# Attention scores of a three-layer kernel: blocks of 32 queries by 96 keys in place of 64 by 128

## The chip, the cores and the metric

One core of a Trainium2 chip runs the whole kernel. The metric is the device time of one execution in microseconds; three executions of the kernel before gave 797.9, 798.71 and 799.32 us, and their median, 798.71 us, is what the change is held against.

## What is computed

The input of two MLP layers is the result of an attention with a sliding window. There are 4 batches, 8 heads, 576 positions and 64 features a head; each position sees itself and the 63 positions before it.

```python
scores = np.matmul(q, k.transpose(0, 1, 3, 2)) / np.sqrt(64)
rel = pos[:, None] - pos[None, :]
scores = np.where((rel >= 0) & (rel < 64), scores, -1e9)
attn = np.exp(scores - scores.max(-1, keepdims=True))
attn = attn / (attn.sum(-1, keepdims=True) + 1e-09)
x = (attn @ v) laid out as [2304, 512]
h = x @ w_in1;  g = np.maximum(h, 0) + alpha * np.minimum(h, 0);  x = g @ w_out1
h = x @ w_in2;  g = h / (1 + np.exp(-h));                         out = g @ w_out2
```

## The kernel before

The 2304 rows are cut into six tiles of 384 rows. The attention works in 24 items: one item is one tile of 384 rows and one pair of heads, whose two times 64 features fill the 128 partitions of `qT` and `kT` (`kT` has 64 keys more, ahead of the tile). An item goes through these functions:

- `mm_s` (S in the opening list, line 212): the scores. For each block of 64 queries (six of them) and each head of the pair there is one fp32 matmul with 64 rows (the features), 64 columns (the queries) and 128 moving columns (the keys from 64 before the block to its end). Each fp32 matmul shows as two instructions in the trace, so an item has 24. The two heads' results lie on the two halves of the partitions (`side`), and even and odd blocks lie in two PSUM banks.
- `peaks` (m, line 223): on VectorE, for each half of an item three instructions that add the mask, scale, write the probabilities' buffer `pr` and take the row's extreme. The bank of a half is given back after its three.
- `exps` (e, line 237): on ScalarE, three exponentials for each half, each with a sum along the row.
- `over` (r) and `scaled` (s): the reciprocal of the sums, and the multiplication by it, on GpSimd (P at the end of the word), ScalarE (A) or VectorE.
- `mm_t` (t, line 272) and `keep_t` (k): three 128 by 128 transposes for each half, and the copy out of PSUM into `pt`.
- `mm_v` (P, line 290): for each of the six blocks and each head one fp32 matmul with 128 rows (the keys), 64 columns (the features of `v`, tiles `vo` and `ve` in turn) and 64 moving columns (the queries): 12 matmuls, 24 instructions.
- `high_v`, `low_v` (x, l): the result is split into two fp32r parts, the input of the first MLP.

The first MLP's first product (`mlp_h1`, M, line 392) takes three fp32r matmuls of 384 columns for each of four 128-row pieces. All items of the first 14, and all M of the first two tiles, stand in an order written out by hand, the string `START`: each word is one call, and the words are issued in that order on every engine's queue (line 811). Among them are q, v and w (loads of queries and keys, of values, of weights), c, h and o (weights taken apart), z (`alpha_in`, line 131: the load of alpha on SyncE's queue, then one VectorE instruction that waits for it), G and J (the MLP's activation).

After the opening the other ten items are done two at a time, every eighth step of the first MLP's loop, in `begin` (line 1052), with five PSUM banks; `soft` spreads their softmax over the next steps. From there on the kernel is the two MLPs alone.

Before the list GpSimd builds the identity and the mask (lines 114 to 127), and for the items 0 to 3 it or VectorE clears the first 64 keys of `kT` (lines 173 and 180: item 0 on VectorE, the others on GpSimd). Keys of the first three items that the list loads go out on ScalarE's queue (line 169), and item 0 is loaded in two halves.

Of the kernel before, what the change touches and what calls it, by code (L numbers as in the profile page):

```python
# [20 lines left out]
q0 q1 q2 S0 m0a S1 e0a q5 q4 m0b e0b r0aP s0aP m1a e1a m1b S2 S5 e1b r0b m2a q3 r1aP m2b e2a r1b s0bP q8 s1bP s1aP t0b  # L21
S3 e2b m5b m5a t1b k0bD m3b q7 v0 S4 e5a r2bP m3a s2bP v1 v2 v5 t0a k1bD m4a r5aP r2aP t1a e5b k1aD k0aD r5bP e3a e4a
S7 S8 m7a e3b e7a t2b s5aP s2aP m8a t5a m4b q6 v6 v4 w12 q9 P0 r3aP r4aP k5aD x0 k2bD s5bP P1 t5b s3aP x1 t2a m7b t3a
e4b k2aD r3bP r7aP S6 s4aP s3bP e7b m8b l0 k5bD P2 t4a m6a s7aP k3a t3b r4bP k3bD t7a r7bP l1 q10 w13 m6b c12a P5 e6a
k7aD s4bP s7bP k4a c12b r6aP P3 t4b c12c t7b e6b r6bP k7b S9 S10 s6aP k4b m9b P7 x5 x3 x2 m10b P4 t6a h12 l2 s6bP t6b
l3 l5 o12 e8a e8b k6b m9a k6aD w3 r8aP w2 z e9a q11 q12 r8bP M0.12.1 M0.12.2 v8 M1.12.1 s8a s8bP P6 m10a x4 c3a x6 t8a
c2a r9a e9b x7 t8b l4 M0.12.3 l6 r9b M0.12.0 l7 s9aP k8a c2b M1.12.0 k8b s9bP t9a e10a c3b c2c r10a M1.12.2 M1.12.3
t9b P8 G1.12 G0.12 k9a S12 S11 c3c v9 k9b h2 h3 J0.12 J1.12 P9 m11a e11a s10aP t10a m11b m12b e11b o2 x9 M0.2.2 M0.2.1
w11 v10 w15 x8 c11a o3 w9 c11b r11a M1.2.1 c13a M1.2.3 M1.2.0 s11a M1.2.2 M1.3.3 M1.3.1 r11b M0.2.3 e10b M0.2.0 M1.3.0
M1.3.2 s11bA v11 q13 l9 r10bP s10bA t10b k10a c11c c9a c13b c9b t11a t11b c15a h11 k10b m12a P10 l8 o11 k11a w14 S13  # L30
c9c k11b P11 w5 c13c h13 m13a c14a x10 x11 M1.11.0 m13b G0.2 c14b M0.3.1 M1.11.2 c15b M0.11.3 l10 M0.3.2 c15c G1.3 h9
v13 w6 M1.11.1 o13D M1.11.3 o9 c14c w7 h15 M1.9.3 l11 M1.9.0 M1.9.2 M0.3.0 v12 w4 M0.3.3 M0.9.1 G1.11 G1.2 G0.3 J1.11
h14 J1.3 J1.2 M1.13.3 o15 M0.11.0 M0.11.2 c6a c5a J0.3 c5b c6b o14 M0.15.1 c4a M1.13.0 M0.15.3 M1.13.1 c5c h5 c4b
M1.9.1 c7a G1.9 M0.15.2 c4c M0.13.2 c7b J0.2 o5D M1.14.2 J1.9 M0.15.0 M1.14.3 M1.13.2 M1.14.1 M0.9.3 G0.15 G1.13 w0 w8
c6c w10 c7c M0.13.0 h7 o7 w1 M1.14.0 J0.15 c0a G1.14 M0.5.1 h4 M0.9.0 h6 J1.14 M0.5.3 M1.15.2 M0.13.1 e13a M1.15.1
M0.5.2 M1.7.1 c10a M1.15.0 M0.14.3 M0.11.1 c10b J1.13 M0.13.3 M1.15.3 M0.9.2 o4 M0.5.0 M1.7.0 G0.13 o6 G0.5 c1a J0.13
c1b G0.11 J0.5 M0.14.2 M1.5.0 M1.7.3 c10c c8a c1c M0.14.1 c8b G0.9 c8c G1.15 M0.14.0 M0.7.2 M1.5.3 M1.5.1 h1 M0.6.1
J0.9 o1D M0.7.1 c0b J1.15 M0.6.2 c0c M1.7.2 M1.5.2 G0.14 h10 J0.11 e12a o10D G1.5 G1.7 e13b h0 h8 o0D M1.4.3 M1.4.2
M0.7.3 J0.14 e12b M0.10.0 M0.4.0 M0.6.0 o8 J1.5 M1.4.1 J1.7 M1.4.0 M1.0.1 M0.6.3 M0.8.2 M0.4.1 G1.4 M0.7.0 M0.4.3
M1.0.3 M1.0.0 M1.0.2 r12a r12bP r13a G0.7 M1.6.1 J1.4 G1.0 G0.6 M1.8.1 M0.8.3 J1.0 M1.1.0 J0.6 M0.10.2 M0.1.3 M1.1.2  # L40
M1.8.0 M0.1.0 M0.1.2 M1.1.1 M1.8.3 M0.1.1 M0.10.3 M1.1.3 J0.7 G0.1 M1.6.0 G1.1 M0.0.0 r13bP M0.4.2 s12bP J1.1 J0.1
M1.8.2 M1.6.3 M1.10.3 M0.0.1 M0.10.1 s13aP G1.8 s12a G0.10 J1.8 J0.10 M0.0.2 M0.8.1 M1.6.2 M0.0.3 M0.8.0 M1.10.1 G0.4
M1.10.0 J0.4 G1.6 G0.0 G0.8 J1.6 J0.0 M1.10.2 s13bP J0.8 G1.10 J1.10
"""


B11, T3, B21, T2, T4, B22, T1 = range(7)
A11, S3, A12, S2, A22, S4, S1, A21 = range(8)
# [3 lines left out]
def attention_two_mlps(ctx, tc, q, k, v, w_in1, w_out1, alpha, w_in2, w_out2, out):  # L52
# [999 lines left out]
    def begin(s, n):  # L1052
# [144 lines left out]
```

## Time and profile before

| | us |
|---|---|
| median of three executions | 798.71 |
| the profiled execution, its time | 800.73 |
| its span, first to last instruction | 798.9 |
| TensorE matmul busy | 787.3 |
| VectorE busy | 631.6 |
| ScalarE busy | 489.3 |
| GpSimd busy | 125.3 |

The profiled execution took 2.0 us (0.25%) more than the median, and 1.8 us of its time lie around the span. Matmuls overlap in the array, and the ends that the profile gives them are modelled; so the length of one says little, and the distance from one start to the next says what it costs. PEclk is the clock that TensorE was granted, as a share of 2.4 GHz.

### The profile page before, as it was taken

Reading aid. Unit: us, or ns where it says so; the run is one execution under the profiler, and the core shown is the slowest. Engines: PE = TensorE matmul, PEld = TensorE weight load, DVE = VectorE, ACT = ScalarE, POOL = GpSimd, SP = SyncE. Lnnn points to the kernel's source line nnn. Section 1 sums busy time; section 2 is a strip of 40 time slices with the busy share of each in tenths; the row PEclk is TensorE's granted clock in tenths of the full one; section 3 lists DMA queues with packets and bytes.
Section 4 is the critical chain, followed back from the end, with each engine's and each line's share of the span. In section 5 each row is a group of like instructions: output and inputs, shape, how many; then the busy total and the mean of one; then the engine's idle time right before and its main releaser. Section 6 shows DMA issues by size and latency. Waiting matters only on the chain.

```text
span 798.9 us, 16657 instructions
## 1 busy us (share of the span) xinstructions
PE 787.3 (99%) x5475; PEld 756.1 (95%) x5475; DVE 631.6 (79%) x1611; ACT 489.3 (61%) x1301; POOL 125.3 (16%) x165
## 2 busy tenths in 40 slices
PE   7899999999999999999999999999999999999998
PEld 6799999999999999999999999999999888888887
DVE  6896647788878998978889775865984988968876
ACT  7873446776734576564577666645766675555553
POOL 6532200000000033132132000000000331311410
PEclk9999999999999999999999999999999999999999
DMA  9878546889676869999998675695758997958922
GB/s 307 284 224 267 179 155 237 299 261 308 207 254 208 279 143 271 287 232 235 282 253 206 206 253 189 224 336 193 228 189 271 296 278 211 209 127 234 208 49 74
DMA packets 126151, 182.79 MB, mean 229 GB/s; under 512 B 12976, under 2 KB 112048, under 8 KB 126064
## 3 DMA queue, kind: packets, MB, share of 16 engines
q1 hardware_dynamic: 111664, 162.25, 61.6%
q0 software_dynamic: 13824, 18.88, 14.3%
q8 instruction: 43, 0.70, 0.4%
q10 hardware_dynamic: 576, 0.59, 0.2%
q14 instruction: 44, 0.36, 0.1%
HBM read 105.52 MB, written 57.28 MB: 204 GB/s over the span
## 4 chain that ended last, share of the span: by engine, by line
PE 91%; DMA 5%; DVE 3%; SPq 1%; issue 0%; ACTq 0%; POOL 0%; ACT 0%; DVEq 0%
PE acc L496 22%; PE h L400 21%; PE acc L695 15%; PE qa L575 12%; PE acc L699 7%; PE qd L575 6%; PE qb L575 3%; PE pa L300 1%; DMA s<-in_moe_w_in_dram 1%; DMA kT<-in_k_dram 1%; PE pa L278 1%; PE pa L220 1%; DMA alpha_sb<-in_moe_alpha_dram 1%; DVE cva L339 1%; DMA ve<-in_v_dram 1%; DVE cva L336 1%
## 5 line engine op out<-in xcount | busy, mean ns | idle before, releaser
L400 PE MATMUL h<-x,i 128*128 128x384 f32 x1152 | 204.8, 337 | 0.6 <-DVE i L372 0.4
L400 PEld LDWEIGHTS h<-x,i 128*128 128x128 f32 x1152 | 200.4, 189 | 1.9 <-DVE i L372 0.7
L695 PE MATMUL acc<-w,gh 128*128 128x512 f32 x489 | 169.2, 394 | 0.0
L496 PE MATMUL acc<-gh,o 128*128 128x384 f32 x672 | 143.5, 334 | 0.0
L699 PE MATMUL acc<-w,gl 128*128 128x256 f32 x489 | 134.3, 277 | 0.0
L346 ACT CAST gh<-gf 128x384 fp32r<-128x384 f32 x168 | 86.0, 515 | 58.0 <-PE acc L496 51.9
L496 PEld LDWEIGHTS acc<-gh,o 128*128 128x128 f32 x672 | 118.9, 188 | 0.0
L695 PEld LDWEIGHTS acc<-w,gh 128*128 128x128 f32 x489 | 91.1, 188 | 20.6
L575 PE MATMUL qa<-v,w 128*128 128x384 f32 x576 | 107.9, 334 | 0.0
L347 DVE TENSOR_TENSOR gl<-gf,gh 128x384 fp32r<-128x384 f32 x168 | 91.6, 553 | 17.8 <-ACT gh L346 14.2
L575 PEld LDWEIGHTS qa<-v,w 128*128 128x128 f32 x576 | 100.6, 188 | 0.0
L346 ACT CAST gh<-g 128x384 fp32r<-128x384 f32 x124 | 63.7, 514 | 55.1 <-PE acc L695 49.2
L699 PEld LDWEIGHTS acc<-w,gl 128*128 128x128 f32 x489 | 91.8, 188 | 0.8
L406 ACT ACTIVATE a<-h 128x384 f32<-128x384 f32 x96 | 45.8, 488 | 73.8 <-PE h L400 70.9
L455 POOL DMA_DIRECT2D gf<-gf x48 | 42.1, 944 | 289.1 <-DMA gf<-g 219.6
L496 PE MATMUL acc<-gl,o 128*128 128x384 f32 x336 | 85.2, 334 | 0.0
L654 POOL DMA_DIRECT2D g<-g x40 | 34.8, 885 | 277.9 <-DMA g<-c 192.3
L347 DVE TENSOR_TENSOR gl<-g,gh 128x384 fp32r<-128x384 f32 x124 | 67.1, 553 | 13.9 <-ACT gh L346 13.6
L415 DVE SCALAR_TENSOR_TENSOR a<-a,nalpha,h 128x384 f32<-128x384 f32 x96 | 57.4, 607 | 17.0 <-ACT a L406 17.0
L243 ACT ACTIVATE pr<-pr,nm 128x128 f32<-128x128 f32 x144 | 56.0, 392 | 10.6 <-DVE nm L231 10.5
L496 PEld LDWEIGHTS acc<-gl,o 128*128 128x128 f32 x336 | 60.6, 188 | 0.0
L575 PE MATMUL qd<-v,w 128*128 128x384 f32 x288 | 57.6, 334 | 0.0
(104 smaller groups left out, 1113.0 us busy)
## 6 DMA issues: line engine op xcount, KB each, us to landing
g<-a SPq DMA_DIRECT2D x96, 192.0 KB, 4.3
gf<-g SPq DMA_DIRECT2D x96, 192.0 KB, 4.0
g<-c SPq DMA_DIRECT2D x96, 192.0 KB, 3.3
g<-g SPq DMA_DIRECT2D x96, 192.0 KB, 4.3
s<-in_moe_w_in_dram SPq DMA_DIRECT2D x32, 512.0 KB, 5.8
s<-in_moe_w_out_dram SPq DMA_DIRECT2D x32, 512.0 KB, 5.2
gf<-gf POOLq DMA_DIRECT2D x48, 192.0 KB, 5.3
g<-g POOLq DMA_DIRECT2D x40, 192.0 KB, 4.0
```

The costliest lines, as they stand in the source:

```text
L243: nc.scalar.activation(out=pr[:, j, :], in_=pr[:, j, :], func=AF.Exp, bias=it[f"nm{hf}"][:, j:j + 1], scale=-1.0, accum_out=it["sm"][:, hf ...
L346: nc.scalar.copy(hi, src)
L347: lows.append(lambda: nc.vector.tensor_tensor(out=lo, in0=src, in1=hi.bitcast(F32), op=ALU.subtract))
L400: nc.tensor.matmul(h, w[:, kk, :], x, start=not done and n == 0, stop=len(done) == KD - 1 and n == 2)
L406: nc.scalar.activation(out=a, in_=begun[t, f][1], func=AF.Relu, scale=-1.0)
L415: nc.vector.scalar_tensor_tensor(out=a, in0=a, scalar=nalpha[:, f:f + 1], in1=h, op0=ALU.mult, op1=ALU.add)
L455: nc.gpsimd.dma_start(out=o, in_=g1[u, b, c], accum_op=ALU.add)
L496: nc.tensor.matmul(o[i], w[:, a, i * P:(i + 1) * P], b, start=start and a == 0 and b is gh, stop=c == KH - 1 and b is gl, skip_group_check ...
L575: nc.tensor.matmul(o, w[:, a, k0], b, start=start and kk == 0 and n == 0, stop=kk == 1 and n == 2, skip_group_check=True)
L654: nc.gpsimd.dma_start(out=gb[u, a, c], in_=gb[u, b, c], accum_op=ALU.add)
L695: nc.tensor.matmul(acc2[u, v][i], gh[:, i * P:(i + 1) * P], w.rearrange("p a d -> p (a d)"), start=first, stop=final, skip_group_check=True)
L699: nc.tensor.matmul(acc2[u, v][i][:, :HD], gl[:, i * P:(i + 1) * P], w[:, 0, :], start=False, stop=final, skip_group_check=True)
```

## The change

The scores are computed in blocks of 32 queries by 96 keys, 12 blocks and two heads an item: 24 fp32 matmuls of 64 rows, 32 columns and 96 moving columns. `home` says where the result of block b and head e lies: which half, which place in it, and which 32 partitions. Places alternate between the two banks, so each bank is read by both halves, and both are given back after the second half's `peaks`. The probabilities' buffers stay 128 wide; the 32 columns that a block leaves out are cleared once for each buffer (`clear`), and buffers are kept apart by half. `peaks`, `exps` and the scaling on ScalarE work on 96 columns; transposes, the copy out of PSUM and the scaling on GpSimd and VectorE stay as they were. In `mm_v` the 64 queries of a block come from two places of `pt`. Where both lie in one half they are one strided operand, as before in number; for two of the six blocks they lie in different halves, and each is a matmul of 32 moving columns with the same 64 columns of `v`: 16 matmuls an item. The mask is built for 32-row groups with eight selects on GpSimd; one pair of variants is copied on GpSimd, the other on VectorE ahead of the first `peaks`. Item 0 is loaded in pieces of 256 and 128 columns. In `begin` the second half's `peaks` of the first coming item are issued with the first half's. The list `START` is a new one, with the same calls in another order.

```diff
 START = """
-q0 q1 q2 S0 m0a S1 e0a q5 q4 m0b e0b r0aP s0aP m1a e1a m1b S2 S5 e1b r0b m2a q3 r1aP m2b e2a r1b s0bP q8 s1bP s1aP t0b
...
-l3 l5 o12 e8a e8b k6b m9a k6aD w3 r8aP w2 z e9a q11 q12 r8bP M0.12.1 M0.12.2 v8 M1.12.1 s8a s8bP P6 m10a x4 c3a x6 t8a
...
+q1 q2 S1 m1a m1b q0 S2 S0 m2a m0a z q5 e1a e1b r1b r1aP e2a q6 q3 S5 q4 q7 r2aP m2b m0b S6 e0a e2b v0 v2 v1 q8 v5 v4
...
+P6 h8 l5 l3 m9a S10 s8aP s8bA m9b t8a w9 x7 w14 t8b x6 l0 x4 o8 q11 c9a e9a e9b l7 c10b l4 M0.8.1 k8a M0.8.0 M0.8.2
...
+    QB = W // 2
+    KW = W + QB
...
+    mask = const.tile([P, 5, KW], F32, name="mask")
+    nc.gpsimd.memset(mask[:, 0, :], 0.0)
+    for p in range(0, P, QB):
+        m = mask[p:p + QB, 0, :]
+        nc.gpsimd.affine_select(out=m, in_=m, compare_op=ALU.is_gt, fill=NEG, base=0, pattern=[[1, KW]],
+                                channel_multiplier=-1)
+        nc.gpsimd.affine_select(out=m, in_=m, compare_op=ALU.is_ge, fill=NEG, base=W, pattern=[[-1, KW]],
+                                channel_multiplier=1)
+    def variants(m, engine):
+        engine.tensor_copy(mask[:, 1 + 2 * m:3 + 2 * m, :], mask[:, :1, :].to_broadcast([P, 2, KW]))
+        for par in range(2):
+            engine.memset(mask[m * W:(m + 1) * W, 1 + 2 * m + par, :W - QB * par], NEG)
+    variants(1, nc.gpsimd)
...
+    def clear(i, engine):
+        s = prs[i] = room(i, [P, HB, P], F32, "pr")
+        flat = s.rearrange("p b c -> p (b c)")
+        for c in ((slice(0, QB), slice(P + KW, 2 * P + QB)) if i % 2 else (slice(KW, P + QB), slice(2 * P + KW, 3 * P))):
+            engine.memset(flat[:, c], 0.0)
...
-        for jb in range(NB):
-            o = jb * W
+        for b in range(2 * NB):
+            o = b * QB
             for e in range(2):
                 r = slice(e * W, (e + 1) * W)
-                nc.tensor.matmul(it["sc"][jb % 2][side(jb, e), jb // 2, :], it["qT"][r, o:o + W],
-                                 it["kT"][r, o:o + P], start=True, stop=True)
+                g = home(b, e)[2]
+                nc.tensor.matmul(it["sc"][b % 2][g * QB:(g + 1) * QB, b // 4, :], it["qT"][r, o:o + QB],
+                                 it["kT"][r, o:o + KW], start=True, stop=True, tile_position=(e * W, g * QB))
...
+    def home(b, e):
+        j, m, par = b // 4, b // 2 % 2, b % 2
+        hf, blk = divmod(2 * j + par, HB)
+        return hf, blk, 2 * m + (e ^ par)
...
-        give("bank", it["scb"][hf])
+        if hf:
+            for i in it["scb"]:
+                give("bank", i)
...
-            for e in range(2):
-                r = slice(e * W, (e + 1) * W)
-                nc.tensor.matmul(pb[r, jb * W:(jb + 1) * W], vt[:, r],
-                                 it[f"pt{hf}"][:, j, side(jb, e)], start=True, stop=True)
+            (h0, b0, _), (h1, b1, _) = (home(2 * jb + i, 0) for i in range(2))
+            parts = [(h0, 0, 2)] if h0 == h1 else [(h0, 0, 1), (h1, 1, 1)]
+            for hf, first, count in parts:
+                for e in range(2):
...
+                    o = jb * W + first * QB
+                    nc.tensor.matmul(pb[r, o:o + count * QB], vt[:, r], rhs, start=True, stop=True)
...
+    for i in spare["pr0"] + spare["pr1"]:
+        clear(i, nc.vector)
...
             mm_s(x)
             if x == n + 2:
                 softmax(x, 0)
+                peaks(x, 1)
```

## Rows read from the trace of the kernel before

**Rows 1.** The page: busy time, share of the span and instructions of each engine.

```profile
PE 787.3 (99%) x5475; PEld 756.1 (95%) x5475; DVE 631.6 (79%) x1611; ACT 489.3 (61%) x1301; POOL 125.3 (16%) x165
```

**Rows 2.** Windows of 20 us: length, then busy time (instructions) by engine, clock, DMA.

```profile
0.00:20.00 20.00, 14.78 (x262) 12.11 (x263) 13.34 (x103) 15.83 (x75) 12.38 (x35) 1.00 0.93 307
20.00:40.00 20.00, 17.49 (x274) 15.46 (x273) 17.17 (x83) 16.73 (x69) 11.70 (x18) 0.91 0.88 283
...
60.00:80.00 20.00, 19.83 (x115) 19.42 (x114) 13.83 (x26) 7.34 (x19) 5.81 (x5) 1.00 0.80 266
80.00:100.00 20.00, 19.59 (x112) 19.27 (x113) 13.78 (x30) 9.63 (x31) 4.19 (x6) 1.00 0.52 178
100.00:120.00 20.00, 20.00 (x199) 19.56 (x199) 8.71 (x25) 9.18 (x27) 0.00 (x0) 1.00 0.47 156
```

**Rows 3.** Groups by line and shape, TensorE: scores, and half the products (busy us, mean ns).

```profile
L220 PE MATMUL pa<-kT,qT 64*64 64x128 f32 x576 | 22.2, 301 | 5.3 <-DMA kT<-in_k_dram 5.3
L300 PE MATMUL pa<-pt,vo 128*64 128x64 f32 x288 | 18.7, 227 | 0.2 <-DMA vo<-in_v_dram 0.2
```

**Rows 4.** Timeline of TensorE, 5 to 16 us: start, length of the merged run.

```profile
5.95 4.12 PE L220 MATMUL pa<-kT,qT 64*64 64x128 f32 x72 [1.00 <-DMA kT<-in_k_dram]
...
12.32 0.55 PE L278 MATMUL pa<-ident,pr 128*128 128x128 f32 x3
12.80 0.89 PE L220 MATMUL pa<-kT,qT 64*64 64x128 f32 x24
13.62 0.88 PE L278 MATMUL pa<-ident,pr 128*128 128x128 f32 x6
14.42 1.54 PE L220 MATMUL pa<-kT,qT 64*64 64x128 f32 x48
```

**Rows 5.** Timeline of TensorE, 24 to 25.3 us: second and last of twelve runs of four.

```profile
24.09 0.29 PE L300 MATMUL pa<-pt,ve 128*64 128x64 f32 x4
...
25.26 0.29 PE L300 MATMUL pa<-pt,ve 128*64 128x64 f32 x4
```

**Rows 6.** Timeline of GpSimd and TensorE, 1 to 5 us: first mask select, `kT` border, first scores.

```profile
1.62 0.29 POOL L119 TENSOR_SCALAR_AFFINE_SELECT mask<-mask 64x128 f32<-64x128 f32 x1
...
2.90 0.23 POOL L180 MEMSET kT<- 128x64 f32 x2
...
3.36 1.60 PE L220 MATMUL pa<-kT,qT 64*64 64x128 f32 x24 [3.36 <-DMA kT<-in_k_dram]
```

**Rows 7.** Timeline of ScalarE: first and last of 36 exponentials in a row.

```profile
5.40 0.40 ACT L243 ACTIVATE pr<-pr,nm 128x128 f32<-128x128 f32 x1 [1.50 <-DVE nm L231]
...
19.05 0.39 ACT L243 ACTIVATE pr<-pr,nm 128x128 f32<-128x128 f32 x1
```

**Rows 8.** Groups by line and shape, ScalarE: one operation at two widths (mean ns second).

```profile
L346 ACT CAST gh<-gf 128x384 fp32r<-128x384 f32 x168 | 86.0, 515 | 58.0 <-PE acc L496 51.9 <-DMA gf<-g 1.6 <-DVE gl L347 1.1
L346 ACT CAST w<-w 128x256 fp32r<-128x256 f32 x77 | 30.3, 402 | 0.9 <-DMA w<-w_i 0.9
```

**Rows 9.** Timeline of SyncE's queue, VectorE and TensorE, 26 to 35 us.

```profile
26.59 1.10 SPq L132 DMA_DIRECT2D alpha_sb<-in_moe_alpha_dram  x1
...
34.20 0.17 DVE L133 TENSOR_SCALAR nalpha<-alpha_sb 128x16 f32<-128x16 f32 x1 [2.11 <-DMA alpha_sb<-in_moe_alpha_dram]
...
34.95 1.54 PE L278 MATMUL pa<-ident,pr 128*128 128x128 f32 x6 [1.43 <-DVE pr L269]
```

**Rows 10.** A window of 3 us: columns as in rows 2.

```profile
36.00:39.00 3.00, 3.00 (x12) 3.00 (x11) 2.93 (x9) 1.69 (x8) 1.66 (x2) 0.50 0.90 266
```

**Rows 11.** Timeline of TensorE and VectorE around one `begin`, 113 to 117 us.

```profile
113.36 1.54 PE L220 MATMUL pa<-kT,qT 64*64 64x128 f32 x48
...
114.28 0.29 DVE L231 CUSTOM_DVE_ANT_0 pr<-pa,mask 128x128 f32<-128x128 f32 x1 [0.98 <-PE pa L220]
...
114.70 0.29 DVE L231 CUSTOM_DVE_ANT_0 pr<-pa,mask 128x128 f32<-128x128 f32 x1
...
116.33 1.24 DVE L316 TENSOR_TENSOR x<-pa,x 128x384 fp32r<-128x384 f32 x2 [1.33 <-ACT x L310]
```

More of the change, by code (lines that the diff above doesn't have):

```diff
@@ L31 @@
[L31 to L40, printed above, removed]
@@ L44 @@
+G0.13 M1.3.1 J0.11 J1.7 M1.3.0 M0.1.1 M1.3.2 M0.1.3 M1.3.3 G0.1 J0.1 J0.13 J1.0 G1.3 J1.3
 """
@@ L114, in attention_two_mlps @@
     make_identity(nc, ident)
[L115 to L127 removed]
+    mask = const.tile([P, 5, KW], F32, name="mask")
[11 more added lines that the diff above has]
+    variants(1, nc.gpsimd)
+    first = ["mask"]
     alpha_sb = const.tile([P, KF], F32, name="alpha_sb")
@@ L140, in attention_two_mlps @@
     AHEAD = 3 * NHP
-    spare = {"pr": [*range(28, 34), 36, 37], "pt": [38, 39, 34, 35], "bank": list(range(8))}
+    spare = {"pr0": [28, 30, 32, 36], "pr1": [29, 31, 33, 37], "pt": [38, 39, 34, 35], "bank": list(range(8))}
+    prs = {}
+    def clear(i, engine):
[3 more added lines that the diff above has]
+            engine.memset(flat[:, c], 0.0)
     def take(kind):
@@ L149, in give @@
             kind = "pr"
-        if kind != "pr" or i > 33 or n < NHP:
-            spare[kind].append(i)
+        if kind == "pr":
+            kind = f"pr{i % 2}"
+            if i < 34 and n >= NHP:
+                return
+        spare[kind].append(i)
     def item_tile(n, x, shape, place):
@@ L171, in load_qk @@
         if n == 0:
-            half = TN // 2
             nc.vector.memset(kt[:, :W], 0.0)
-            for c in (slice(0, half), slice(half, TN)):
+            for c in (slice(0, 2 * P), slice(2 * P, TN)):
                 nc.sync.dma_start(out=qt[:, c], in_=q[rows, c])
@@ L266, in scaled @@
             for j in range(HB):
-                nc.scalar.activation(out=pr[:, j, :], in_=pr[:, j, :], func=AF.Copy, scale=rs[:, j, :])
+                p = pr[:, j, keys(hf, j)]
+                nc.scalar.activation(out=p, in_=p, func=AF.Copy, scale=rs[:, j, :])
         else:
@@ L1065, in begin @@
         for i, x in enumerate(coming):
-            for d, what in ((0, lambda x=x: softmax(x, 0)), (1, lambda x=x: softmax(x, 1)), (1, lambda x=x: load_qk(x + 2)),
+            for d, what in ((0, lambda x=x: softmax(x, 0)), (1, lambda x=x, i=i: softmax(x, 1) if i else exps(x, 1)), (1, lambda x=x: load_qk(x + 2)),
                             (2, lambda x=x: over(x, (0, 1))), (3, lambda x=x: scaled(x, 0, True)),
```

82 lines of the change are left out of this document (46 added, 36 removed).

## The prediction

> **What bounds the kernel now.** I read the page's busy times first: TensorE is busy 787.3 of 798.9 us [rows 1], so the end moves by what its own work costs and by what little it waits. The windows of 20 us say where the 11.6 idle us are: 5.2, 2.5, 0.2 and 0.4 us in four windows of the first 100 us, 8.3 together, and none from 100 us on [rows 2]. So there are two accounts. In the first some 40 us TensorE waits for loads, softmax and weights, and the new list and the cheaper softmax can change that. Everywhere else each nanosecond that the attention's matmuls gain or lose on TensorE is a nanosecond of the kernel; VectorE, ScalarE and GpSimd have slack there.
>
> Next, what those matmuls cost. An item's scores are 24 instructions (576 in 24 items [rows 3]). Their mean of 301 ns says nothing, since they overlap; the timeline gives the pace: a run of 48 lasts 1.54 us and one of 24 lasts 0.89 us, so an item adds 0.65 us, 27.1 ns an instruction, and each run has 0.24 us of ends and change-over [rows 4]. Three more transposes lengthen a run from 0.55 to 0.88 us: 0.11 us for 128 columns on the whole array [rows 4]. A score has a quarter of the array (64 by 64) and as many columns, and costs a quarter of that. Four tiles do run side by side, and the cost goes by share of the array times columns. The products with v (288 with `vo` [rows 3] and as many with `ve`) start in runs of four, 0.117 us apart (ten steps from 24.09 to 25.26 [rows 5]): 29.2 ns each, 0.70 us an item. By share and columns they would take 0.11/4 = 27.5 ns.
>
> **The change part by part.**
> Scores: 48 instructions on an eighth of the array with 96 columns. If share times columns still holds, an item takes 0.65 x 96/128 = 0.49 us: 0.16 less, and 24 items give **-3.9 us**. Bounds: below, the run's ends of 0.24 us shrink by a quarter too, 24 x 0.06 = 1.4 more; above, 48 at today's 27.1 ns = 1.30 us, +15.6 us. I take -3.9: today's pace is what the streaming of the columns alone would give, so nothing else yet limits it at four instructions in 0.11 us.
>
> Products with v: four of the six blocks keep their four instructions. Two blocks get eight with 32 columns. From below: half the columns, half the time, 0. From above: eight at the pace of four in 0.117 us, +0.117 us a block, +0.23 an item, **+5.6 us** in 24. I take the upper end. At 64 columns the pace is already 6% above what the streaming gives, where scores and transposes sit on it; so something that does not shrink with the moving columns seems to set it, and each of the new instructions loads the same 64 columns of v as before.
> The Trainium skill ("TensorE: Matmul & The Clock Gate", section LDWEIGHTS) speaks against this part: the time of a weight load goes by its columns, 64/1.2 = 53 ns here, whatever is streamed. By it two tiles side by side would need 53 ns for two instructions, and the part would cost 24 x 2 x 0.107 = 5.1 us (an estimate from that page); no run here has 32 moving columns.
>
> Start: GpSimd's first mask select begins at 1.62, and two `kT` borders follow at 2.90; the first scores wait for a load until 3.36 [rows 6]. The new list begins with item 1, whose border is cleared by GpSimd, behind eight selects of 0.29 us (four before) and the copy and two fills of a mask variant. Four selects more are 1.2 us less what narrower ones save, and the copy some 0.3: the border is ready near 4.4, so the first scores start **+1.1 us** late (bounds 0 and 1.4). The 16 fills of buffers and the other variant are VectorE's, which has nothing to do until the first scores are done; without that cover the fills, at the 0.11 us of one border [rows 6], would cost 1.8 us once.
>
> Softmax: ScalarE runs 36 exponentials without a pause, 0.39 us apart, from 5.40 to 19.05 [rows 7]: the opening's first third is its. The same engine takes 515 ns for 384 columns and 402 for 256 [rows 8], 0.88 ns a column, so 32 fewer save 28 ns; 60 exponentials by the first M make 1.7 us. TensorE feels it only where it idles on them: the idle 5.2 + 2.5 less the first 3.36 is 4.4 us, of which 1.4 is the next part's. Of the other 3.0, waits for loads stay (1.0 at 5.95 [rows 4] is one), so I take **-0.5** (bounds 0 and -1.7). VectorE's shorter `peaks` lie under ScalarE's stream.
>
> Alpha: its load is issued at 26.59 behind weight loads, and VectorE waits for it 2.11 us to 34.20; the next scaling is late, and TensorE's transposes sit idle 1.43 us before 34.95 [rows 9]. Then the clock is at 0.50, the 1.2 GHz level, from 36 to 39 [rows 10]; at full clock that work takes 1.5 us. The new list has z eleventh, and SyncE has four loads ahead of it: it lands while the first `peaks` still run. So **-1.4 and -1.5 us**, unless another stall takes the place: the new list puts other calls in the same queues, and what is late next then is a weight load or ScalarE, whose 60 exponentials before the first M alone are 23 us at 0.39. Bounds 0 and -2.9. Opening together: 1.1 - 0.5 - 1.4 - 1.5 = **-2.3 us**; bounds -4.6, everything well, and +3, the late start and a stall of the old size elsewhere on top.
>
> `begin`: `mm_v` of the second item takes a bank that is now free only after five `peaks` instead of three. Scores begin at 113.36, and VectorE's three start 0.21 us apart, end at 115.0, and it idles until 116.33 [rows 11]. Two more end by 115.4; the product, behind two items' scores (0.98), their ends (0.24) and the first item's product (0.93), starts near 115.5. Cost 0, under VectorE's idle time, with 0.1 us to spare: without that cover five times some 0.3 us.
>
> Sum: -3.9 + 5.6 - 2.3 = -0.6 us. The sum is against the profiled execution, 800.73 us (span 798.9 and 1.8 around it), which would come to 800.1. That execution stands 2.0 us above the median of the runs; carried over to the median, 798.71 - 0.6 = **798.1 us**.
>
> **The rivals.**
> *Weight loads hide.* The split blocks cost by columns, 0 in place of +5.6: 798.7 - 3.9 - 2.3 = **792.5**, faster. For it: no stall on loads shows in scores or transposes. Against: the 6%.
> *Only four tiles run side by side*, as now, because four column tiles that share the same 64 rows may not stream at once; it ends slower. Then four instructions take 0.11 x 96/128 = 0.081 us, 48 take 0.98, +0.33 an item, +7.8: 798.7 + 7.8 + 5.6 - 2.3 = **809.8**. Against: today two column tiles on the same rows do run at once. It decides from 12 ns an instruction on: there 48 take 0.58 us and the sum is +1.6.
> *Instructions come no faster than today's*, 27.1 ns: +15.6 + 5.6 - 2.3, **817.6**. Against: the pace fits the streaming, so it is no sign of a limit. The Trainium skill ("TensorE: Matmul & The Clock Gate", section "Wait — 56ns, not 53.3ns?") gives this rule: start to start never below about 25 ns, however few columns. By it 48 would take 1.2 us and the time be some 815 (an estimate from that page). Rows average 27.1 and go no lower, so they leave it open.
>
> **How the numbers follow.** A measurement of this kernel tells about 0.2% (1.6 us) from no change, so faster means under 797.1 and slower above 800.3. Forecast 0.68, its own range 795.8 to 803.4 from the opening's bounds; loads hide 0.19; four tiles 0.08; pace 0.05. The forecast lies 1.0 us above the lower limit and 2.2 under the upper, and the opening decides, worth some 2.5 us either way: 0.24 of its 0.68 faster, 0.32 same, 0.12 slower. Rival one is all but wholly faster (0.18, 0.01 same); the others slower (0.13). Faster 0.42, same 0.33, slower 0.25. The range, 791.0 to 803.4, takes in rival one with most of its opening's bounds and leaves out the two slow ones.
>
> **What would show it.** Runs of L220: 48 instructions adding 0.49 us (0.65, 0.98, 1.2 or more: the rivals). The products: eight instructions of a split block in 0.23 us against 0.117. First scores near 4.4 us; exponentials 0.36 us apart; no wait on alpha and no stretch at 0.50 near 36 us; no TensorE idle from 100 us on, else `begin` has lost its cover. The prediction is wrong if scores don't fall to 0.49, if split blocks cost nothing, or if the new list idles TensorE over 4 us more or less than I count.

## The result, and the profile after

The changed kernel takes **807.85 us** (median of four executions, 807.61 to 813.3) against 798.52 us for the kernel before beside it on the same chip: a ratio of 1.0131 (of the means, with a fifth execution of 808.65 us in it), 95% interval 1.0094 to 1.0168. It is slower by 9.3 us, and the prediction, 798.1 us within 791.0 to 803.4, was wrong.

The profiled execution is the slowest of the four (813.3 us, span 811.5). The clock column of its windows of 20 us is 0.91 in two of them, 20 to 40 and 60 to 80: each time behind one of the two longest stalls below, the clock is at 1.2 GHz for 3.4 us. Its mean granted clock is 0.996, that of the others 1.000 (0.998 in the fifth), so these stretches are not in the median. First the page: busy times and the queue that carries TensorE's instructions; it had 43 packets and 0.70 MB before.

```profile
PE 794.1 (98%) x6243; PEld 762.3 (94%) x6243; DVE 634.1 (78%) x1633; ACT 487.9 (60%) x1318; POOL 120.5 (15%) x165
...
q8 instruction: 49, 0.80, 0.4%
```

TensorE has 768 matmuls more and 6.8 us more busy time [rows 1]; the rest of the 12.6 us that the span grew is idle time.

The first question is where in the span the loss lies. One line of the timeline answers it, the first matmul of the second product of the first MLP, behind which there is no attention:

```profile
283.13 0.85 PE L539 MATMUL acc<-gh,o 128*128 128x384 f32 x4
```

From there to the end it is 528.4 us here, and 528.0 to 528.2 in the traces of before and of the first four experiments (e1 to e4). So all of the loss stands ahead of this point, in the opening list and in `begin`.

TensorE's timeline around one `begin` answers to [rows 3, 5, 11]. First, from before, where two items' products begin and what follows them; then after, where the line below "..." is the last run of products:

```profile
114.83 0.34 PE L300 MATMUL pa<-pt,vo 128*64 128x64 f32 x4
...
116.38 1.83 PE L400 MATMUL h<-x,i 128*128 128x384 f32 x9
```

```profile
121.05 1.40 PE L237 MATMUL pa<-kT,qT 64*32 64x96 f32 x96
122.38 0.34 PE L344 MATMUL pa<-pt,vo 128*64 128x64 f32 x4
122.54 0.29 PE L344 MATMUL pa<-pt,ve 128*64 128x64 f32 x4
122.66 0.38 PE L344 MATMUL pa<-pt,vo 128*64 128x32 f32 x8
122.86 0.40 PE L344 MATMUL pa<-pt,ve 128*64 128x32 f32 x8
123.10 0.31 PE L344 MATMUL pa<-pt,vo 128*64 128x64 f32 x4
...
124.17 0.29 PE L344 MATMUL pa<-pt,ve 128*64 128x64 f32 x4
124.39 12.76 PE L443 MATMUL h<-x,i 128*128 128x384 f32 x72
```

Two items' products take from 122.38 to 124.39, 2.01 us; before they took 1.55 (from 114.83 to 116.38). That is +0.23 us an item. The runs of eight start 0.20 and 0.24 us apart, 0.22 where four took 0.117 [rows 5]. Two items' scores last 1.40 us; one item's, in the next fence, lasts 0.83. So an item adds 0.57 us, where it added 0.65 [rows 4] and 0.49 was predicted.

TensorE's timeline in the opening (start, length, and in brackets the idle time ahead and what ended it):

```profile
5.02 2.17 PE L237 MATMUL pa<-kT,qT 64*32 64x96 f32 x96 [5.02 <-POOL kT L196]
...
13.76 3.44 PE L314 MATMUL pa<-ident,pr 128*128 128x128 f32 x15
...
20.83 1.20 PE L314 MATMUL pa<-ident,pr 128*128 128x128 f32 x9
...
29.57 0.85 PE L314 MATMUL pa<-ident,pr 128*128 128x128 f32 x6 [2.26 <-POOL sm L294]
...
34.67 0.83 PE L237 MATMUL pa<-kT,qT 64*32 64x96 f32 x48
...
67.03 15.77 PE L443 MATMUL h<-x,i 128*128 128x384 f32 x81 [2.01 <-issue]
83.57 36.23 PE L443 MATMUL h<-x,i 128*128 128x384 f32 x207 [0.76 <-DVE a L458]
...
212.39 0.36 PE L344 MATMUL pa<-pt,ve 128*64 128x32 f32 x5 [1.33 <-issue]
```

Read it in this order. The first scores start at 5.02 us, not 3.36 [rows 6]. Fifteen transposes at 13.76 take 3.44 us, 0.23 each, where three more cost 0.33 in before [rows 4]: half pace, though the listed clock is 1.00 there. The kernel before is at full pace by 12.32 us [rows 4]. The trace's own records of the clock explain the 1.00: they begin only at 17.0 us in after and at 11.8 us in before, and where there is no record the column prints 1.00. The pace doubles just where they begin (transposes start 213 ns apart ahead of 17.0 us and 109 ns behind it; in before, instructions of the scores 54 and 25 ns). So by its pace TensorE is at the 1.2 GHz level up to there. That this lasts to 17.0 us is not a mark of the changed kernel: in e2 and f1 (below), with the same instructions up to there, the records begin at 8.2 and 9.9 us. Then come idle stretches that the kernel before doesn't have: 2.26, 2.01, 0.76 and 1.33 us.

### The profile page after: what moved, and what is told of

It is laid out like the page before. It is cut to its first block, busy times and chain, and to the rows that moved or that the text cites. A ratio compares the mean times of both kernels' runs of the same rounds, so it can differ in the third digit from the quotient of the medians.

```text
span 811.5 us, 18205 instructions
## 1 busy us (share of the span) xinstructions
PE 794.1 (98%) x6243; PEld 762.3 (94%) x6243; DVE 634.1 (78%) x1633; ACT 487.9 (60%) x1318; POOL 120.5 (15%) x165
## 4 chain that ended last, share of the span: by engine, by line
PE 95%; DMA 2%; issue 1%; DVE 1%; ACT 1%; POOL 0%; SPq 0%; ACTq 0%; DVEq 0%
PE h L443 23%; PE acc L539 22%; PE acc L738 14%; PE qa L618 12%; PE acc L742 7%; PE qd L618 6%; PE qb L618 3%; PE pa L344 3%; PE pa L314 2%; PE pa L237 2%; DMA kT<-in_k_dram 1%; DMA g<-a 1%; ACT pr L279 0%; DVE i L415 0%; POOL pr L305 0%
## 5 line engine op out<-in xcount | busy, mean ns | idle before, releaser
L279 ACT ACTIVATE pr<-pr,nm 128x96 f32<-128x96 f32 x144 | 52.1, 366 | 8.0 <-DVE nm L265 8.0
```

Of the source, the lines that this page charges most:

```text
L279: nc.scalar.activation(out=p, in_=p, func=AF.Exp, bias=it[f"nm{hf}"][:, j:j + 1], scale=-1.0, accum_out=it["sm"][:, hf * HB + j:hf * HB + ...
```

## The experiments

Each ratio is to the kernel before, run in the same batch on the same chip.

**e1_new_list_old_blocks: the list alone.** Functions and blocks of before, the string `START` of after.

```diff
-q0 q1 q2 S0 m0a S1 e0a q5 q4 m0b e0b r0aP s0aP m1a e1a m1b S2 S5 e1b r0b m2a q3 r1aP m2b e2a r1b s0bP q8 s1bP s1aP t0b
+q1 q2 S1 m1a m1b q0 S2 S0 m2a m0a z q5 e1a e1b r1b r1aP e2a q6 q3 S5 q4 q7 r2aP m2b m0b S6 e0a e2b v0 v2 v1 q8 v5 v4
...
```

> The functions of the kernel before with the new opening list. Theory A (the blocks): the 9.3 us come from TensorE's own account, split products +5.6, scores only -1.7 as instructions arrive some 16 ns apart, and from waits that the denser instructions bring; then the list with the old blocks costs little: 797 to 801 us. Theory B (the list): the order of the opening is what is slow; then 803 to 806 us.

804.11 us, 1.0077 (1.0062 to 1.0092): the list by itself costs 6.1 us, with TensorE's work untouched. The list is more than an order: 33 of its 525 calls also go to another engine than before (the reciprocal `r0aP` on GpSimd is now `r0a` on VectorE, for instance), which the description of the change leaves out. e1 carries both, so the order and the choice of engines are not told apart. Its timeline shows matmuls that wait for joins of the MLP's activation, which free a bank: 0.76 us ahead of a matmul of the MLP and 1.32 us ahead of the first `begin`:

```profile
77.12 36.26 PE L400 MATMUL h<-x,i 128*128 128x384 f32 x207 [0.76 <-DVE a L415]
114.70 1.50 PE L278 MATMUL pa<-ident,pr 128*128 128x128 f32 x12 [1.32 <-DVE a L415]
...
274.15 0.85 PE L496 MATMUL acc<-gh,o 128*128 128x384 f32 x4
```

**e2_products_whole: the split undone.** After, with the two split blocks multiplied as one operand of 64 columns, taken from the first two blocks of the first half's buffer; the 64 queries of those blocks then get other rows' probabilities.

```diff
-            parts = [(h0, 0, 2)] if h0 == h1 else [(h0, 0, 1), (h1, 1, 1)]
+            if h0 != h1:
+                b0, b1 = 0, 1
+            parts = [(h0, 0, 2)]
```

> The changed kernel, but the two blocks of 64 queries whose halves lie apart are multiplied as one matmul each with probabilities from the first half's buffer; those two blocks' output is left out of the computation in that sense. 24 instructions an item in place of 32. Theory A: 24 items times 0.23 us, 5.6 us less than 807.9: about 802.3. If other engines set the pace and the split blocks are hidden: 807 to 808.

804.43 us, 1.0083 (1.0054 to 1.0113): 6.5 us over the before of its batch, 2.9 less than the 9.3 of after, with executions from 802.3 to 807.64. The direction is the expected one; the size, 5.6 expected, lies inside that spread.

**e3_border_on_vector: the late start undone.** After, with the first 64 keys cleared on VectorE.

```diff
-            nc.gpsimd.memset(kt[:, :W], 0.0)
+            nc.vector.memset(kt[:, :W], 0.0)
```

> The changed kernel with the border of kT for items 1 to 3 cleared on VectorE in place of GpSimd, so that the first scores need not wait for the masks until 5.0 us. If the late start goes through to the end: 1.3 to 1.7 us less than 807.9, about 806.4. If ScalarE, loads or weights set the opening's end: 807.4 to 808.4.

807.7 us, 1.0117 (1.0102 to 1.0132). The first scores start at 4.13 in place of 5.02, and the end doesn't move. What starts earlier waits longer for a later load of keys (1.71 us, to 11.20; 0.84 in after):

```profile
4.13 2.28 PE L237 MATMUL pa<-kT,qT 64*32 64x96 f32 x96 [4.13 <-DMA kT<-in_k_dram]
...
11.20 2.31 PE L237 MATMUL pa<-kT,qT 64*32 64x96 f32 x96 [1.71 <-DMA kT<-in_k_dram]
```

**e4_old_alpha_early: the alpha wait undone.** Before, with z moved to the eighth place of its own list.

```diff
-q0 q1 q2 S0 m0a S1 e0a q5 q4 m0b e0b r0aP s0aP m1a e1a m1b S2 S5 e1b r0b m2a q3 r1aP m2b e2a r1b s0bP q8 s1bP s1aP t0b
+q0 q1 q2 S0 m0a S1 e0a z q5 q4 m0b e0b r0aP s0aP m1a e1a m1b S2 S5 e1b r0b m2a q3 r1aP m2b e2a r1b s0bP q8 s1bP s1aP t0b
...
```

> The kernel before with the load of alpha (z) moved from just ahead of the first M to the eighth place of its old list. If VectorE's wait of 2.1 us for alpha costs TensorE its 1.4 us of idle and the half clock behind it, as the prediction's step says: 1.4 to 2.9 us less than 798.5, about 796. If another wait takes its place: 798 to 799.

798.55 us in ten executions, 1.0013 (1.0001 to 1.0024): no gain. Its trace has neither the wait of 1.43 us ahead of the transposes nor the stretch at half clock. But the early load makes a wait of its own: VectorE stands 1.41 us for alpha, to 7.24 us, and TensorE waits longer ahead of its first transposes. The first line is from before, the second from e4:

```profile
10.41 0.90 PE L278 MATMUL pa<-ident,pr 128*128 128x128 f32 x3 [0.34 <-POOL pr L269]
11.35 0.55 PE L278 MATMUL pa<-ident,pr 128*128 128x128 f32 x3 [1.18 <-POOL pr L269]
```

So e4 by itself does not say what the old wait was worth.

**e5_old_keys_in_two and e9_old_products_split: more instructions under the old list.** Before, each with one edit.

```diff
-                nc.tensor.matmul(it["sc"][jb % 2][side(jb, e), jb // 2, :], it["qT"][r, o:o + W],
-                                 it["kT"][r, o:o + P], start=True, stop=True)
+                for c in (slice(0, W), slice(W, P)):
+                    nc.tensor.matmul(it["sc"][jb % 2][side(jb, e), jb // 2, c], it["qT"][r, o:o + W],
+                                     it["kT"][r, o + c.start:o + c.stop], start=True, stop=True)
```

> The kernel before, its list and blocks kept, but each scores matmul of 64 queries by 128 keys written as two of 64 keys: the same columns are streamed, with 48 weight loads and 48 matmuls an item in place of 24 and 24. Theory A (instruction supply): instructions limit TensorE in two ways. Pace: one weight load and matmul every 16.6 ns, seen in the changed kernel where its queue had run dry, so an item's scores take 48 x 16.6 = 0.80 us against 0.65, +0.15 x 24 = +3.5 us. Fetch: the instructions come in packets of 16 KB, 256 instructions each; with 1152 more (some 4 or 5 packets more than the 43) some packet should land after the instructions ahead of it are used up, in a stretch with busy DMA queues before 220 us, and TensorE stand for about 1.4 us beyond its landing, in all 0 to 4 us. Sum 802 to 806 us. Rival B (columns alone count): the same 799 us within 1 us, no stall that the profile calls issue.

```diff
-            for e in range(2):
-                r = slice(e * W, (e + 1) * W)
-                nc.tensor.matmul(pb[r, jb * W:(jb + 1) * W], vt[:, r],
-                                 it[f"pt{hf}"][:, j, side(jb, e)], start=True, stop=True)
+            for c in ((0, 32), (32, 64)) if jb in (2, 3) else ((0, 64),):
+                for e in range(2):
+                    r = slice(e * W, (e + 1) * W)
+                    u = side(jb, e).start
+                    nc.tensor.matmul(pb[r, jb * W + c[0]:jb * W + c[1]], vt[:, r],
+                                     it[f"pt{hf}"][:, j, u + c[0]:u + c[1]], start=True, stop=True)
```

> The kernel before, its list and its scores kept; in the products the third and fourth of the six blocks are written as two halves of 32 columns each, so an item issues 32 product matmuls in place of 24, as the changed kernel does. Theory A (the prediction's own term, +0.23 us an item on TensorE, and nothing else of weight, since only 384 instructions or 1.5 packets are added): +5.5 us, 803.0 to 805.0 us. Rival B (half of the items stand in the first 60 us, where TensorE also waits for loads and softmax, and part of the added time fills those waits): +2 to +4 us, 800.3 to 802.3 us. Rival C (stalls for instructions come on top, as they did with the scores cut in two): 805 to 809 us.

e5: 807.42 us, 1.0119 (1.0087 to 1.015), above the 802 to 806 of theory A. e9: 805.97 us, 1.0100 (1.0082 to 1.0118), in rival C's range, but without rival C's stalls. e5's rows, the two runs with one and with two items' scores, and two waits:

```profile
13.15 1.03 PE L221 MATMUL pa<-kT,qT 64*64 64x64 f32 x48
...
28.45 0.49 PE L279 MATMUL pa<-ident,pr 128*128 128x128 f32 x3 [1.39 <-POOL sm L260]
28.86 1.77 PE L221 MATMUL pa<-kT,qT 64*64 64x64 f32 x96
...
35.09 0.34 PE L301 MATMUL pa<-pt,ve 128*64 128x64 f32 x4 [3.49 <-issue]
```

An item adds 0.74 us instead of 0.65, for the same columns: +0.09, or 2.2 us in 24 items. The other 7 us of e5 are not TensorE's own work. The longest wait is TensorE standing 3.49 us for nothing that the profile shows, and the clock is at 1.2 GHz for 3.4 us behind it. e5's executions differ in the clock: 805.3 and 805.69 us have a mean granted clock of 0.996 and 0.998, 809.15 and 809.76 us have 0.993. e9's products cost what the prediction said, 0.23 us an item or 5.5 us; 3.0 us come on top. It has no stall put down to issue. It waits longer for loads (1.89 us to 6.89, 1.94 us to 41.55), and 1.6 of the 3.0 us are a wait for ScalarE in the second MLP, far behind the attention:

```profile
518.70 1.31 PE L577 MATMUL qa<-v,w 128*128 128x384 f32 x6 [1.62 <-ACT fk L582]
```

Whether e9's other executions have this wait too is not known.

**What "issue" is.** The trace lists the packets by which each instruction queue is filled. Before has 43 of 16 KB on q8 and 11064 records of TensorE, after 49 and 12586; 256 records a packet in both, so one record is 64 bytes and q8 is TensorE's. In the traces of all these runs, every stall put down to issue begins when TensorE has used its 449th record plus a multiple of 256, and ends 1.2 to 1.7 us after a packet has landed. In after the two long ones begin behind record 2497 (8 x 256 + 449) and 5569 (20 x 256 + 449). The 2.26 us before 29.57, which the profile puts down to GpSimd, begin behind record 1217 (3 x 256 + 449), so they are one of these as well; so are 3.80 us in e2 that it puts down to VectorE, and the 1.39 us in e5 above, which make 5.4 us there with 3.49 and 0.56. Before, e1, e4, e6, e7, e9 and f2 have none. The window from 64.6 to 65.7 us, ahead of the matmul at 67.03, shows the packet and the data that moves beside it:

```profile
DMA packets 65, 0.21 MB, mean 195 GB/s; under 512 B 15, under 2 KB 16, under 8 KB 64
...
q1 hardware_dynamic: 64, 0.20, 45.2%
q8 instruction: 1, 0.02, 5.5%
```

The earliest packets of a run start when TensorE has used record 155 to 160 plus a multiple of 256, so there are some 290 records between the earliest start and the need. (The packet in this window starts at 64.65 us; TensorE had used record 2208, 8 x 256 + 160, at 59.37.) At two a matmul and 0.57 us for 48 matmuls that is 1.7 us of scores, and 25 us of MLP matmuls at 0.17 us. In the kernel before a packet also starts up to 6 us after TensorE has reached record 160 (the first one: 8.58 and 14.50 us), and still lands before the need, since its items use up records more slowly.

**f1_new_half_v and f2_old_half_v: fewer bytes ahead of the packets.** After and before, with half of the bytes of the early loads of v; the third and fourth pair of heads are multiplied with the values of the first two. One of the edit's two places:

```diff
-                nc.sync.dma_start(out=s[lost:], in_=v[t0 + c * P + lost:t0 + c * P + P])
+                nc.sync.dma_start(out=s[lost:, :HD], in_=v[t0 + c * P + lost:t0 + c * P + P, :HD])
...
```

> The changed kernel without half of the early loads of v: for the first two groups of tokens only the columns of the first two head pairs are loaded (128 KB in place of 256 KB a tile, 2 MB less in the first 45 us), and the other two head pairs multiply with those. All instructions of all engines stay. Theory A (TensorE stands for instruction packets because these wait behind data on the DMA queues, 3 to 5 us each before 70 us): with less data ahead of them the packets come earlier, the stall at 27 us goes and the one at 65 us shrinks, 803 to 805.5 us, a gain of 2.5 to 5 us, while the kernel before gains less than 1.5 us by the same edit, as it has no such stall. Rival B (the packets are asked for too late whatever the queues hold, or the loss stands in the engines): within 1 us of after.

> The kernel before with the same edit: half of the early loads of v left out, and the third and fourth head pair multiplied with the values of the first two. It stands for what the loads alone give: TensorE waits for kT, ve and vo for 2.9 us in all in the first 30 us of before. Theory A (no stall for instructions there, and the softmax engines set the pace behind the loads): 797 to 798 us, a gain under 1.5 us. Rival B (the loads set the pace of the first 40 us): 794 to 796 us, and then a gain of the changed kernel by the same edit says nothing of instruction packets.

f1: 806.92 us, 1.0108 (1.0084 to 1.0131). f2: 797.61 us, 0.9992 (0.9978 to 1.0005). TensorE's waits by releaser, f1:

```profile
PE h L443 <- issue: 1.3, 3, 0.6
PE pa L314 <- POOL pr L305: 1.0, 1, 1.0
PE h L443 <- DVE a L458: 0.8, 1, 0.8
...
PE pa L344 <- issue: 0.3, 1, 0.3
```

and after:

```profile
PE pa L314 <- POOL sm L294: 2.3, 1, 2.3
PE h L443 <- issue: 2.0, 1, 2.0
PE pa L344 <- issue: 1.6, 2, 1.3
```

The stalls of this kind shrink: 2.6 us in f1 (1.03, 0.56, 0.40, 0.34 and 0.32), 6.4 us in the profiled execution of after, 4.4 us in e3, whose profiled execution stands near its median. That speaks for data ahead in the queues as what delays the packets, with one trace of each. But the time hardly follows: f1 is 0.9 us under after, and the kernel without such stalls gains 1.0 us by the same edit. The 2.5 to 5 us that I expected are not there. The stalls are part of the loss at most for their own 2 to 4 us, and for the clock where it falls behind them; and e1, without any, loses 6 us as well.

**f3_old_both_split and e11_new_list_keys_in_two: do the parts add up?** f3 is before with the edits of e5 and e9 together, e11 is e1 with the edit of e5.

> The kernel before, with its list, and both edits that give TensorE the changed kernel's instruction count: scores matmuls in two of 64 keys, and two of the six product blocks in halves of 32 columns. Alone they cost 9.2 and 8.5 us. Theory A (the new list is a gain once TensorE has the new count of instructions, and only with the old blocks does it cost 6 us): the two add up nearly, 813 to 816 us, well above the 807.9 us of the changed kernel. Rival B (the costs overlap in the same waits, and the new list gives nothing): 807 to 811 us.

> The new list with the old blocks, each scores matmul written as two of 64 keys (the edit that cost 9.2 us with the old list). Theory A (list and instruction supply add up): 804.3 + 9.2 = 812 to 815 us. Rival B (they overlap: while TensorE stands for instructions, VectorE, ScalarE and the loads catch up, and the waits of the list shrink, as they are shorter in the changed kernel than in the new list with old blocks): the pace term of 24 x 0.12 = 2.8 us and little more, 805.5 to 809 us.

f3: 812.62 us, 1.0174 (1.0152 to 1.0195). e11: 809.28 us, 1.0150 (1.0135 to 1.0166). Both lie between their theories, below the sum of the parts (816 and 813). f3 does not say that the new list is a gain: its scores cost 0.74 us an item and those of after 0.57, and 24 times that, 4.1 us, is nearly all of the 4.8 us between them.

Put together, TensorE's own account (scores +0.09 or -0.08 us an item, products +0.23, times 24) against what was measured, in us over the before of the same batch:

| kernel | list | own account | measured | beyond it |
|---|---|---|---|---|
| after | new | +3.6 | +9.3 | 5.7 |
| e1, old blocks | new | 0 | +6.1 | 6.1 |
| e2, no split | new | -1.9 | +6.5 | 8.4 |
| e11, keys in two | new | +2.2 | +11.8 | 9.6 |
| e4, z early | old | 0 | +0.6 | 0.6 |
| e5, keys in two | old | +2.2 | +9.2 | 7.0 |
| e9, products split | old | +5.5 | +8.5 | 3.0 |
| f3, both | old | +7.7 | +14.0 | 6.3 |

Only the old list with the old blocks runs without 3 to 10 us on top. In the rows of e5 and f3 a part of it is time at the lower clock: f3's executions have a mean granted clock of 0.994 to 1.000, and the one at 1.000 takes 811.02 us. In e1 all executions are at 0.999 or 1.000, and in after all but the profiled one at 0.998 or more.

**e7_joins_early: the late joins of e1.** e1 with `J1.6` ahead of `c11a`, and `t10a t10b` behind `M0.12.1`.

```diff
-J1.10 J1.14 c11a J1.6 r13b
+J1.10 J1.14 J1.6 c11a r13b
...
-J0.10 t10a t10b M0.9.1 M0.9.2 M0.12.1
+J0.10 M0.9.1 M0.9.2 M0.12.1 t10a t10b
```

> The kernel with the old blocks and the new list, two places of the list changed: the join of chunk 6 of the second part ahead of a weight conversion on VectorE, and the two transposes of item 10 behind three MLP words. In the trace of the new list with old blocks TensorE waits 0.76 us at 76.4 and 1.32 us at 113.4 for a join on VectorE to free a bank. Theory A (the new list costs its 6 us over before in part by such late joins): both waits go, 804.1 - 2.1 = 802 us. Rival B (another wait takes their place, because the next bank is as late): 803.5 to 804.5 us.

804.78 us, 1.0086 (1.0065 to 1.0107): no gain, and both waits are still in the trace (0.76 us to 81.26, 1.32 us to 118.81). The words that I moved were not the ones that these matmuls wait for; the 1.32 us stand behind the last join of the list. What the joins cost is therefore not measured.

**e6_old_warm, e8_new_warm and e10_old_warm_short: the half pace at the start.** Matmuls whose results nobody reads, at the head of TensorE's queue: ten f32 ones in before, sixteen in after, and ten bf16 ones in before. The edit of e6:

```diff
+    warm = const.tile([P, P], F32, name="warm")
+    nc.vector.memset(warm, 0.0)
+    for _ in range(10):
+        nc.tensor.matmul(bank(7, "warm")[:, :P], warm, warm, start=True, stop=True)
```

> The kernel before with ten matmuls of a cleared 128 by 128 tile at the head of TensorE's queue, into a bank that nothing has used yet. In the trace of before TensorE runs at half pace up to about 10.4 us (72 scores matmuls in 4.12 us against 24 in 0.89 later) although the granted clock is listed as 1.00. Theory A (the pace rises a while after TensorE has begun, whatever it does): the matmuls run from about 1 to 3.4 us, the pace rises some 2 us earlier, and about 1 us of TensorE's time is gained, of which the waits for loads keep part: 797.5 to 798.5 us. Rival B (DMA and the softmax engines set the pace of the first 40 us): no change within 0.3 us. Rival C (the added matmuls delay the first scores or shift the instruction packets for the worse): up to +1 us.

> The changed kernel with sixteen matmuls of the identity with itself at the head of TensorE's queue, into a bank that nothing has used yet; nothing else differs. In the trace of after TensorE works at half pace up to about 17 us (15 transposes in 3.44 us against 9 in 1.20 later), in before up to about 10.4 us. Theory A (the longer half pace is a part of the loss): they run from about 1.4 to 5 us, the pace rises near 10 us, transposes at 13 us take 0.13 us each and not 0.23, and 1.5 to 3 us are gained: 805 to 806.5 us. Rival B (the softmax engines and the loads are late by as much, and TensorE only waits longer): within 0.7 us of after. The 32 instructions more also move every later instruction against its packet, so single stalls for instructions may come or go, by up to 2 us each.

> The kernel before with ten bf16 matmuls of a cleared tile, 128 by 128 weights and 256 columns, at the head of TensorE's queue, into a bank that nothing has used yet. The ten f32 ones of the run before this took 8.48 us at half pace and so held up the first scores by 6 us; these should end by 3.4 us, when the first operands land. Theory A (work of another kind brings full pace earlier): the scores after 6 us run at full pace, the first transposes come before 9 us, 796.5 to 798 us. Rival B (the pace rises some 7 us after the first scores whatever stands ahead of them, as in the run before this): 72 scores matmuls again take about 4.1 us, and the time is that of before within 0.7 us.

e6: 803.57 us, 1.0066 (1.0046 to 1.0086). e8: 824.48 us, 1.0317 (1.0292 to 1.0342). e10: 801.39 us, 1.0055 (1.0039 to 1.0072). All three miss as tests of what the half pace costs, because the added matmuls are slow themselves and hold up the scores. The first lines of the timeline of e6:

```profile
1.05 8.48 PE L116 MATMUL warm<-warm 128*128 128x128 f32 x20 [1.05 <-DVE warm L114]
9.46 4.92 PE L224 MATMUL pa<-kT,qT 64*64 64x128 f32 x96
16.36 0.55 PE L282 MATMUL pa<-ident,pr 128*128 128x128 f32 x3 [1.99 <-POOL pr L273]
```

They do say that 8.48 us of work ahead of the scores doesn't bring the full pace at once: 96 scores matmuls take 4.92 us, where 48 at full pace take 1.54 [rows 4], and the clock's records begin at 13.7 us. With the bf16 ones 72 take 3.13 us (4.12 before), and the records begin at 9.2 us; but without any added matmul they begin at 8.6 us in e1 and 10.4 in e9, so this can be chance. e10 loses 3.9 us. Its scores start 1.9 us late, and its transposes at 18.82 us wait 1.57 us, which begin behind record 449: a late packet. e8's trace has five stalls behind such records, 9.6 us together.

**e12_new_shifted: half a packet earlier.** After, with 32 small matmuls (128 records) at the head.

```diff
+    for _ in range(32):
+        nc.tensor.matmul(bank(7, "shift")[:32, :8], ident[:32, :32], ident[:32, :8], start=True, stop=True)
```

> The changed kernel with 32 matmuls of 32 by 32 by 8 at the head of TensorE's queue, 128 instructions or half a packet, which should end before the first scores can start at 5.0 us. In all runs so far every stall that is put down to issue began when TensorE had used up its 449th instruction plus a multiple of 256. Theory A (those stalls are late instruction packets): they leave the places that they have in the changed kernel (27.3, 65.0 and 211 us, all at the words that follow instruction 449 plus a multiple of 256), and those that come are again at such a number, counted with the added ones, so half a packet earlier in the work; the time moves by up to 3 us either way. Rival B (they belong to the places, to busy DMA queues or to the words there): they stay at the same words within a few matmuls, and the time is that of after within 0.7 us.

816.8 us, 1.0250 (1.0203 to 1.0297). They last 10.4 us, not 3, and the scores start at 11.69, so the time says nothing. The places do. The stalls of after at 27, 65 and 211 us are gone, and the new ones begin at records 449, 705 (256 + 449) and 3521 (12 x 256 + 449), counted with the added ones:

```profile
17.95 2.77 PE L239 MATMUL pa<-kT,qT 64*32 64x96 f32 x126 [2.17 <-issue]
22.90 0.36 PE L239 MATMUL pa<-kT,qT 64*32 64x96 f32 x5 [2.18 <-issue]
...
126.43 0.36 PE L346 MATMUL pa<-pt,ve 128*64 128x32 f32 x6 [0.60 <-issue]
```

So the stalls belong to the number of records, not to the words of the list or to busy queues alone. The scores of e12 also start 6.7 us later than those of after, among other loads; what that does to the stalls is not separated.

## Why the prediction was wrong

*Products, +5.6: right.* Eight instructions take 0.22 us in after, in e9 and in f3 alike, the upper end that was taken. The Trainium skill ("TensorE: Matmul & The Clock Gate", section LDWEIGHTS) was weighed here with 53 ns a weight load; the trace agrees nearly, with 55 ns for each of the four pairs of tiles in 0.22 us. The prediction says that this page speaks against the part; by the prediction's own estimate from it, +5.1, it speaks for it.

*Scores, -3.9: the sign right, the size half.* 0.57 us an item and not 0.49, so -1.9. The step "share times columns still holds" failed in part. In the trace groups of eight start 0.08 us apart for the first four groups, as predicted; from then on mostly one weight load with its matmul follows every 16.6 ns. What limits it there was not tested. e5 confirms it without any change of columns: 48 instead of 24 matmuls for the same columns add 0.09 us. The rivals with four tiles (0.98) and with today's pace (1.30) fell. The rule of the Trainium skill (same page, section "Wait — 56ns, not 53.3ns?") with which the last of them was given, never below some 25 ns from start to start, does not hold for tiles side by side: 48 matmuls in 0.57 us are 11.9 ns each.

*Opening, -2.3: this is the step that failed.* With products and scores as measured the own account is +3.6, and what is left of the 9.3, +5.7, stands in the opening, with 1 to 2 us of it in `begin`. Its terms, one by one:

- *Alpha, -1.4 and -1.5.* The wait is gone from after; what that gave can't be read from its total. The half clock was a feature of the profiled execution, which stood 2.0 us above the median: its mean granted clock is 0.998, and that of the 40 executions of before beside the experiments is 0.999 or 1.000, all but one (0.997). The wait varies too: with z in its old place TensorE waits there 0.29 us in e10 and 0.35 in f2, and not at all in e6 and e9, each of which changes something else in the opening. I took both terms out of that one execution and carried the difference over to a median that hardly contains them. The wait in e10:

```profile
34.93 1.23 PE L282 MATMUL pa<-ident,pr 128*128 128x128 f32 x6 [0.29 <-DVE pr L273]
```

- *Late start, +1.1.* It is 1.66 us, and e3 shows that 0.9 us of it is worth nothing at the end. The later start was foreseen, and the step from TensorE's idle time to the end was wrong.
- *ScalarE, -0.5.* Exponentials start 0.36 us apart, as predicted, with no gain to be seen.
- *The list itself, 0.* I costed a new order by the waits that it removes, and bounded what it adds at one stall of the old size. e1 puts it at 6.1 us. Where it lies is seen when TensorE's time, from one start to the next, is summed by the kind of matmul that it last started, up to the first matmul of the second product (us, one trace each, all at full clock behind the start):

| kernel | ahead of the first | scores | transposes | products | MLP, first product |
|---|---|---|---|---|---|
| e4, old list | 3.4 | 24.1 | 19.1 | 20.4 | 201.2 |
| e1, new list, old blocks | 4.1 | 24.1 | 19.5 | 20.9 | 205.5 |
| e3, new list, new blocks | 4.1 | 22.0 | 19.7 | 27.4 | 204.8 |
| e9, old list, products split | 3.4 | 23.9 | 20.3 | 25.8 | 201.2 |

With both kinds of blocks most of what the new list loses stands behind the MLP's 1152 matmuls (e3's products, +7.0, are the 5.5 of their own account and a packet's stall of 1.81 us). Other old-list traces reach 202.5 there (f2, e10), so it is 2 to 4 us: 0.76 us for a join on VectorE in both, 1.32 us ahead of `begin` in e1, the late packets in e3, and many too short to show in a row. In e9 the sum does not grow.

*`begin`, 0: right as far as it can be seen.* Peaks of the second half follow those of the first 0.18 us apart. Behind 100 us TensorE waits 1.81 us in e3, for a packet; in after 1.33 us for a packet and 0.53 us, to 137.68, for a join. (The prediction's "none from 100 us on" passes over 3.3 us of idle time in the last 14 us of before. Nothing rests on it.)

What stays open: which waits make the 3 to 10 us "beyond" in each row of the table. The late start, late joins and late packets are each in traces of the changed kernel with 1 to 4 us, but taking one away or making it shorter (e3, f1), or trying to (e7), gave back little; in e3 another wait was ready behind it. No version that does the whole work beats the kernel before. The new blocks with the old list were not run: that order has up to six first halves waiting at a time, and the new blocks have four buffers for each half. So what the new list costs or gains with the new blocks is argued from e1 and f3, not shown.

## What to carry to other kernels

An order written out by hand may hold only for the durations under it. Cost a change of such an order, or of a duration under it, as TensorE's own account plus an unknown of several us, and give that unknown a sign: here it was 3 to 10 us to the bad every time but one, and never a gain. Count instructions beside columns when a matmul is cut into smaller ones, for their pace (11.9 ns each here) and for the records that have to be fetched. And before you credit a stall of the profiled execution, see whether the median contains it; the granted clock of the other executions is a first sign.

## What the runs showed of the hardware

- TensorE runs out of instructions: 256 records of 64 bytes a packet, needed by record 449 plus a multiple of 256, and usable 1.2 to 1.7 us after landing. With six packets more after has stalls of 2.26, 2.01, 1.33 and 0.43 us and two smaller ones; the profile calls them issue, but for the longest, which it puts down to GpSimd.
- The clock can fall behind a stall: in after it is at 1.2 GHz for 3.4 us from 30.6 and from 68.2 us, behind the stalls that end at 29.57 and 67.03, and in e5 from 35.4 us, behind the 3.49 us that end at 35.09. The 1.81 us in e3, to 207.33, have no such stretch behind them.
- Eight tiles of 64 by 32 do run side by side (groups of eight start 0.08 us apart), but a long run of them goes by instructions, 16.6 ns for a weight load with its matmul, and not by columns.
- The half pace of the first microseconds does not show in the clock column, which is 1.00 from 0 to 20 us for want of records. The records begin between 8.2 us (e2) and 17.0 us (after) in the traces without added matmuls, and the pace rises there (transposes in after from 213 to 109 ns). 8.48 us of f32 matmuls ahead of the scores didn't end it sooner: in e6 they begin at 13.7 us.
- Ten f32 matmuls of 128 by 128 by 128 take 8.48 us there, 0.42 us for each of their twenty instructions; fifteen transposes of the same size take 0.23 us each in the same state.
